# The first pair of heads by unsplit float32 matmuls of 64 rows, and a first value matmul in two pieces

## The chip, the cores and the metric

The kernel runs on 1 core of one Trainium2 chip. The metric is the device time of one execution in microseconds (us), as the median of several runs. Before the change it is 764.4 us, median of 3 runs (762.76 to 766.11).

## What is computed

Attention in which only the keys within `tau` of the row's largest score keep a weight, then a causal convolution of 5 taps that gives a gate, and two 512x512 products. The shapes are 8 batches, 8 heads, 576 positions and 64 numbers per head, all in float32.

```python
scores = scale * np.matmul(q, k.transpose(0, 1, 3, 2))
thresh = np.max(scores, axis=-1, keepdims=True) - tau
scores = np.where(scores >= thresh, scores, -1000000000.0)
attn = softmax(scores)
x = (attn @ v).transpose(0, 2, 1, 3).reshape(B, S, H * D)
gate = sigmoid(causal_conv5(x, conv_w))
out = (gate * (x @ w_val)) @ w_out
```

## The kernel before

The work is cut into 32 jobs, one for each batch and pair of heads (`Job`). A job has nine tiles of scores (`Tile`), each of 128 rows by 576 keys: four query blocks for each of two heads, and one tile, called both, in which the last 64 queries of both heads share the 128 rows. A tile goes through TensorE (scores, `multiply`, L504), VectorE (negative row maximum, L508), ScalarE (exponential L514 and threshold L516) and VectorE again (keep and sum, L530). Two heads of one query block make a `Group`: it is divided by its sum on GpSimd (L560) or ScalarE (L556), turned by TensorE (L610) and copied to SBUF by ScalarE (L621, L626, L632). Five such groups fill two halves of 320 and 256 queries. For each half `Half.attended` (L653) multiplies the turned weights by the values: five key chunks for each of two heads, where head 0 writes partitions 0 to 63 of the result and head 1 partitions 64 to 127. `convolve` and `products` follow (the taps of the first batch on TensorE, L700, the tap of later batches on GpSimd and VectorE, L740 and L747, the two products on TensorE, L794).

A score is not made of one float32 matmul. `prepare` loads q and k of a pair (`q_r`, `k_r`), scales q (L350) and splits both into a high and a low float32r part (L333, L342 on ScalarE, L292 in two pieces each on GpSimd). DMAs then copy the parts within SBUF so that one matmul of 128 rows adds two of the products of parts (`KH`, `KL`, `Q`), and GpSimd places the last 64 queries on a block diagonal (`bd`, L215) for the tile both. Job 0 has a way of its own, `load_at_once`: eight DMAs on two queues bring q and k of both heads twice from HBM, ScalarE makes the high parts (L432, L433) and VectorE the low ones (L438, L440), head by head. `prepare` is called for job 0 as well, for its tile both alone.

The order of the instructions is not that of the text. Every step is an `op` with an engine, a due time, a cost and a list of what it waits for. `carry_out` then plays the engines against each other with those costs and writes the instructions in the order that results. A change to one early step or cost therefore moves instructions all through the program. Buffers are counted rooms (`r_s`: two tiles of scores in PSUM; `r_pre`: two, of which one is lent out at first for the diagonals of the taps).

```python
for c in (NKC, *range(NKC)):
    for h, hs in enumerate(HEADS):
        ...
        nc.tensor.matmul(
            acc[hs, :w], t.v[:, c0 : c0 + D], T[:, chunk, :],
            start=c == NKC, stop=c == NKC - 1, skip_group_check=True,
        )
```

Of the kernel before, what the change touches and what calls it, by code (L numbers as in the profile page):

```python
# [10 lines left out]
F32 = mybir.dt.float32  # L11
# [4 lines left out]
ALU = mybir.AluOpType  # L16
AX = mybir.AxisListType

P = 128
# [3 lines left out]
DUE = (8, 8, 8)  # L23
# [5 lines left out]
def tile_thresholded_attention_gated_mix(  # L29
# [14 lines left out]
    nc = tc.nc  # L44
# [169 lines left out]
    def spread(dst, src):  # L214
        nc.gpsimd.tensor_scalar(dst, src, 1.0, 0.0, op0=ALU.mult, op1=ALU.add)  # L215
# [85 lines left out]
    class Job:  # L301
# [16 lines left out]

        def prepare(self, due):
            b, g = self.b, self.g  # L320
            copy = self.i > 0

            def fetch_k():
                self.k_r = r_kr.take()
                nc.sync.dma_start(self.k_r, kT[b, g])

            def fetch_q():
                self.q_r = r_qr.take()
                nc.sync.dma_start(self.q_r, qT[b, g])

            def high_k():
                self.kh = r_kh.take()
                nc.scalar.copy(self.kh, self.k_r)  # L333

            def low_k():
                if not hasattr(self, "kl"):
                    self.kl = r_kl.take()
                return self.kl, self.k_r, self.kh

            def high_q():  # L340
                self.qh = r_qh.take()
                nc.scalar.copy(self.qh, self.q_r)  # L342

            def low_q():
                if not hasattr(self, "ql"):
                    self.ql = r_ql.take()
                return self.ql, self.q_r, self.qh

            def scale_q():
                nc.gpsimd.tensor_scalar(self.q_r, self.q_r, sc, 0.0, op0=ALU.mult, op1=ALU.add)  # L350

            got_k = op("SP", due - 6, 0.55, 4.0, fetch_k, takes=[r_kr])
            got_q = op("SP", due - 6, 0.55, 4.0, fetch_q, takes=[r_qr])
            self.high_k = op("ACT", due, 0.62, 0.8, high_k, [got_k], [r_kh])
            self.low_k = subtract(due + 1, SK, low_k, [self.high_k], [r_kl], [(r_kr, lambda: self.k_r)])
            scaled = op("POOL", due, 0.75, 0.86, scale_q, [got_q])
            high = op("ACT", due + 1, 0.58, 0.76, high_q, [scaled], [r_qh])
            low = subtract(due + 2, S, low_q, [high], [r_ql], [(r_qr, lambda: self.q_r)])

            def place(which):  # L360
                def run():
                    if which == 0:
                        self.bd = r_bd.take()
                    for hs in HEADS:
                        src = (self.ql if which else self.qh)
                        spread(self.bd[hs, which, hs], src[hs, 0:SL].bitcast(F32))

                return run

            self.blocks = [op("POOL", due + 3, 0.45, 0.6, place(0), [high], [r_bd])]  # L370
            self.blocks.append(op("POOL", due + 3, 0.45, 0.6, place(1), [low, self.blocks[0]]))
            self.give_q = [(r_qh, lambda: self.qh), (r_ql, lambda: self.ql)]
            self.copied = []
            if not copy:
                self.blocks[1].gives = self.give_q
                return

            def copies(name, rooms, src, r):
                def run():
                    if r == 0:  # L380
                        setattr(self, name, rooms.take())
                    dst, x = getattr(self, name), getattr(self, src)
                    for h, hs in enumerate(HEADS):
                        nc.sync.dma_start(
                            dst[HEADS[r], h, :].bitcast(F32), x[hs, self.window(h)].bitcast(F32)
                        )

                return run

            for name, rooms, src, done in (  # L390
                ("KH", r_KH, "kh", self.high_k), ("KL", r_KL, "kl", self.low_k)
            ):
                o = op("SP", due + 1, 1.1, 3.6, copies(name, rooms, src, 0), [done], [rooms])
                o2 = op("SP", due + 1, 1.1, 3.6, copies(name, rooms, src, 1), [done, o])
                self.copied += [o, o2]

            def copies_q(which):
                def run():
                    if which == 0:
                        self.Q = r_Q.take()  # L400
                    x = (self.ql if which else self.qh)
                    for h, hs in enumerate(HEADS):
                        nc.sync.dma_start(
                            self.Q[HEADS[which], h, :].bitcast(F32), x[hs, SL:S].bitcast(F32)
                        )

                return run

            o = op("SP", due + 2, 1.1, 3.6, copies_q(0), [high], [r_Q])
            last = op("SP", due + 2, 1.1, 3.6, copies_q(1), [low, o, *self.blocks],  # L410
                      gives=self.give_q)
            self.copied += [o, last]
# [5 lines left out]
        def load_at_once(self):  # L418

            b, g = self.b, self.g  # L420
            k2, q2 = r_pp.take(), r_pp.take()
            queues = [nc.sync, nc.scalar]
            for h, hs in enumerate(HEADS):
                for r, queue in zip(HEADS, queues):
                    queue.dma_start(k2[r, h * S : (h + 1) * S], kT[b, g, hs, self.window(h)])
                    queue.dma_start(q2[r, h * S : h * S + NKC * P], qT[b, g, hs, SL:S])
            self.Q, self.KH, self.KL = r_Q.take(), r_KH.take(), r_KL.take()
            self.first = []

            def highs(h):  # L430
                k_r, q_r = k2[:, h * S : (h + 1) * S], q2[:, h * S : h * S + NKC * P]
                nc.scalar.copy(self.KH[:, h, :], k_r)  # L432
                nc.scalar.mul(self.Q[:, h, :], q_r, sc)  # L433

            def lows(h):
                k_r, q_r = k2[:, h * S : (h + 1) * S], q2[:, h * S : h * S + NKC * P]
                Q = self.Q[:, h, :]
                nc.vector.tensor_sub(self.KL[:, h, :], k_r, self.KH[:, h, :].bitcast(F32))  # L438
                lo = HEADS[1]
                nc.vector.scalar_tensor_tensor(  # L440
                    Q[lo], q_r[lo], sc[lo], Q[lo].bitcast(F32), op0=ALU.mult, op1=ALU.subtract
                )

            last = []
            for h in range(2):
                last = [op("ACT", -20, 1.3, 1.5, lambda h=h: highs(h), last)]
                low = op("DVEp", -20, 1.5, 1.6, lambda h=h: lows(h), last)
                if h == 1:
                    low.gives = [(r_pp, lambda: k2), (r_pp, lambda: q2)]
                self.first.append(low)  # L450


    class Tile:
        def __init__(self, k, t, h, qc, grp):
# [1 line left out]
            i = h or 0  # L456
            both = h is None
            if both:
                after = [t.high_k, t.low_k, *t.blocks]
            elif t.i == 0:  # L460
                after = [t.first[h]]
            else:
                after = t.copied
            if tiles:
                after = after + [tiles[-1].scores]
            gives = []
            if t.last == (h, qc):
                gives = [(r_Q, lambda: t.Q), (r_KH, lambda: t.KH), (r_KL, lambda: t.KL)]
            if both:
                gives = [(r_kh, lambda: t.kh), (r_kl, lambda: t.kl), (r_bd, lambda: t.bd)]  # L470
            self.scores = op(
                "PE", k - DUE[0], 0.80 if both else 0.54, 1.06 if both else 0.8, self.multiply,
                after, [r_s], gives,
            )
            largest = op("DVE", k - DUE[1], 0.67, 0.84, self.largest, [self.scores], [r_nm])
            if TH == "ACT":
# [14 lines left out]
        def multiply(self):  # L491
            t, h, qc = self.t, self.h, self.qc
            s = self.s = r_s.take()
            for a in range(2):
                hs = slice(a * HS, (a + 1) * HS)
                if h is None:
                    ks = slice(SL + a * HS, SL + (a + 1) * HS)
                    bd = [t.bd[:, i, :] for i in range(2)]
                    terms = [(bd[0], t.kh[:, ks]), (bd[1], t.kh[:, ks]), (bd[0], t.kl[:, ks])]
# [137 lines left out]
    class Half:  # L637
# [4 lines left out]
        def attended(self, k):  # L642
# [3 lines left out]
            def attend():  # L646
                acc = self.acc = r_acc.take()
                T = self.T[:, :, 0:w]
                for c in (NKC, *range(NKC)):
                    for h, hs in enumerate(HEADS):  # L650
                        c0 = (2 * c + h) * D
                        chunk = 2 * NKC if c == NKC else h * NKC + c
                        nc.tensor.matmul(  # L653
                            acc[hs, :w], t.v[:, c0 : c0 + D], T[:, chunk, :],
                            start=c == NKC, stop=c == NKC - 1, skip_group_check=True,
                        )

            def evacuate():
                if j == 0:
# [223 lines left out]
        nc.gpsimd.memset(t.bitcast(F32), 0.0)  # L883
    for _, t in r_xT.free:
        nc.gpsimd.memset(t[:, 0:PAD], 0.0)
    jobs[0].prepare(-6)
    got_cw = op("SP", -20, 0.1, 5.0, lambda: None)
    last, conv_ready = from_f64(
        lambda: cw_raw, lambda: cw_work[0], cw_work[1], cw_work[2], 1, False, [got_cw]
# [80 lines left out]
```

## Time and profile before

| | |
|---|---|
| median of 3 runs | 764.4 us |
| the profiled execution, its own time | 766.08 us |
| its span, first to last instruction | 763.9 us |
| TensorE (PE) busy | 723.8 us, 95% |
| VectorE (DVE), ScalarE (ACT), GpSimd (POOL) busy | 609.8, 637.0, 552.3 us |
| share of PE in the chain that ended last | 72% |
| DMA, mean over the span | 130 GB/s |

Busy is time in which an instruction of the engine was under way. Matmuls overlap, so the pace of TensorE is read from the starts of its instructions, not from their length. In the rows of the trace a bracket tells how long the engine was idle before the instruction and whose work ended that. PEld is the loading of TensorE's weights, SPq and ACTq are instructions that issue DMAs. PEclk is the granted share of TensorE's clock.

### The profile page before, as it was taken

Reading aid. Unit: us, or ns where it says so; the run is one execution under the profiler, and the core shown is the slowest. Engines: PE = TensorE matmul, PEld = TensorE weight load, DVE = VectorE, ACT = ScalarE, POOL = GpSimd, SP = SyncE. Lnnn points to the kernel's source line nnn. Section 1 sums busy time; section 2 is a strip of 40 time slices with the busy share of each in tenths; the row PEclk is TensorE's granted clock in tenths of the full one; section 3 lists DMA queues with packets and bytes.
Section 4 is the critical chain, followed back from the end, with each engine's and each line's share of the span. In section 5 each row is a group of like instructions: output and inputs, shape, how many; then the busy total and the mean of one; then the engine's idle time right before and its main releaser. Section 6 shows DMA issues by size and latency. Waiting matters only on the chain.

```text
span 763.9 us, 16282 instructions
## 1 busy us (share of the span) xinstructions
PE 723.8 (95%) x5424; PEld 617.2 (81%) x5424; DVE 609.8 (80%) x1292; ACT 637.0 (83%) x1466; POOL 552.3 (72%) x908
## 2 busy tenths in 40 slices
PE   3779999999899999999999999999999999999997
PEld 3557678887788888888878888888898888888897
DVE  5796999986788888888788887888888878888730
ACT  5787989988788989888889899888998889988832
POOL 4988778886679867788558976779678777676531
PEclk9999999999899999999999999999999999999999
DMA  6656656446455465654455556545465456550001
GB/s 186 175 144 152 155 133 165 119 116 172 111 142 125 112 165 140 156 127 122 131 131 140 128 143 157 153 104 145 131 161 128 120 141 156 129 125 18 32 33 62
DMA packets 51890, 99.05 MB, mean 130 GB/s; under 512 B 9056, under 2 KB 9056, under 8 KB 51808
## 3 DMA queue, kind: packets, MB, share of 16 engines
q1 hardware_dynamic: 51488, 97.47, 49.8%
q8 instruction: 43, 0.70, 0.4%
q10 hardware_dynamic: 320, 0.56, 0.3%
q14 instruction: 39, 0.32, 0.1%
HBM read 35.74 MB, written 9.44 MB: 59 GB/s over the span
## 4 chain that ended last, share of the span: by engine, by line
PE 72%; DVE 8%; POOL 7%; ACT 6%; issue 3%; DMA 3%; SPq 1%; POOLq 0%; ACTq 0%; DVEq 0%
PE acc L794 20%; PE acc L653 20%; PE s L504 18%; PE tp L610 13%; DVE pp L530 3%; DVE nm L508 2%; ACT e L514 2%; POOL pp L560 2%; ACT T L621 2%; DVE pre L747 1%; DMA q_r<-qT 1%; POOL gl L292 1%; POOL ql L292 1%; PE acc L700 1%; POOL kl L292 1%
## 5 line engine op out<-in xcount | busy, mean ns | idle before, releaser
L508 DVE TENSOR_REDUCE nm<-s 128x1 f32<-128x576 f32 x288 | 216.1, 754 | 61.6 <-PE s L504 56.6
L514 ACT ACTIVATE e<-s,nm 128x576 f32<-128x576 f32 x288 | 215.9, 750 | 33.8 <-DVE nm L508 19.1
L530 DVE SCALAR_TENSOR_TENSOR pp<-s,nm,e 128x576 f32<-128x576 f32 x256 | 207.3, 813 | 36.1 <-ACT nm L516 33.1
L621 ACT COPY T<-tp 128x384 f32<-128x384 f32 x384 | 176.0, 488 | 23.9 <-PE tp L610 22.4
L610 PE MATMUL tp<-ident,pp 128*128 128x128 f32 x1152 | 179.9, 275 | 6.8 <-POOL pp L560 6.4
L504 PE MATMUL s<-KH,Q 128*128 128x288 f32 x512 | 161.0, 330 | 23.1 <-DVE pp L530 13.8
L653 PE MATMUL acc<-T,v 128*64 128x256 f32 (+1 forms) x1280 | 171.0, 414 | 1.5 <-ACT T L621 1.0
L560 POOL TENSOR_SCALAR pp<-pp,sums 128x576 f32<-128x576 f32 x179 | 145.6, 819 | 32.1 <-DVE sums L549 22.3
L610 PEld LDWEIGHTS tp<-ident,pp 128*128 128x128 f32 x1152 | 140.1, 141 | 11.7 <-POOL pp L560 8.2
L504 PE MATMUL s<-KL,Q 128*128 128x288 f32 x512 | 145.0, 298 | 0.0
L653 PEld LDWEIGHTS acc<-T,v 128*64 128x64 f32 x1280 | 86.8, 137 | 63.9 <-issue 7.9
L504 PEld LDWEIGHTS s<-KH,Q 128*128 128x128 f32 x512 | 98.9, 193 | 45.0 <-DVE pp L530 19.4
L747 DVE SCALAR_TENSOR_TENSOR pre<-xT,cw,pre 128x576 f32<-128x576 f32 x112 | 106.2, 948 | 13.2 <-POOL pre L740 12.9
L504 PEld LDWEIGHTS s<-KL,Q 128*128 128x128 f32 x512 | 98.5, 192 | 0.2
L547 POOL TENSOR_SCALAR sums<-sums 128x2 f32<-128x2 f32 (+1 forms) x160 | 48.8, 305 | 57.1 <-DVE pp L530 40.8
L516 ACT ACTIVATE nm<-nm,less 128x1 f32<-128x1 f32 x288 | 85.2, 296 | 0.0
L794 PE MATMUL acc<-gl,woh 128*128 128x320 f32 (+1 forms) x256 | 78.9, 308 | 2.4 <-POOL gl L292 2.4
L794 PE MATMUL acc<-gh,wol 128*128 128x320 f32 (+1 forms) x256 | 79.1, 309 | 0.0
L794 PE MATMUL acc<-gh,woh 128*128 128x320 f32 (+1 forms) x256 | 78.9, 308 | 0.0
L794 PE MATMUL acc<-xh,wvl 128*128 128x320 f32 (+1 forms) x256 | 78.7, 307 | 0.0
L794 PE MATMUL acc<-xl,wvh 128*128 128x320 f32 (+1 forms) x256 | 78.5, 307 | 0.0
L794 PE MATMUL acc<-xh,wvh 128*128 128x320 f32 (+1 forms) x256 | 78.1, 305 | 0.0
(84 smaller groups left out, 1249.0 us busy)
## 6 DMA issues: line engine op xcount, KB each, us to landing
KH<-kh SPq DMA_DIRECT2D x124, 144.0 KB, 2.5
KL<-kl SPq DMA_DIRECT2D x124, 144.0 KB, 3.6
k_r<-kT SPq DMA_DIRECT2D x32, 320.0 KB, 4.0
v<-vs SPq DMA_DIRECT2D x32, 320.0 KB, 3.2
q_r<-qT SPq DMA_DIRECT2D x32, 288.0 KB, 3.4
outT<-o SPq DMA_DIRECT2D x32, 288.0 KB, 2.1
Q<-qh SPq DMA_DIRECT2D x62, 128.0 KB, 2.2
Q<-ql SPq DMA_DIRECT2D x62, 128.0 KB, 2.4
```

What stands on the lines that cost most here:

```text
L504: nc.tensor.matmul(s[:, a, :HS], w, m, start=i == 0, stop=i == len(terms) - 1)
L508: nc.vector.tensor_reduce(self.nm[:, 0:1], self.s[:, :, :HS], axis=AX.XY, op=ALU.max, negate=True)
L514: nc.scalar.activation(self.e, self.s[:, :, :HS], AF.Exp, bias=self.nm[:, 0:1])
L516: nc.scalar.activation(self.nm[:, 1:2], self.nm[:, 0:1], AF.Identity, bias=less, scale=-1.0)
L530: nc.vector.scalar_tensor_tensor(grp.p[:, i * S : (i + 1) * S].rearrange("p (a f) -> p a f", a=2), self.s[:, :, :HS], self.nm[:, 1:2], self.e,
L547: add = op("POOL", k - 4, 0.2, 0.33, lambda: nc.gpsimd.tensor_scalar(sums(), sums(), 1.0, 1e-9, op0=ALU.mult, op1=ALU.add), [self.kept])
L560: nc.gpsimd.tensor_scalar(v, v, ri(i), 0.0, op0=ALU.mult, op1=ALU.add)
L610: nc.tensor.transpose(tp[:, i * P : (i + 1) * P], self.p[:, k0 : k0 + P], ident)
L621: nc.scalar.copy(T[:, c0 : c0 + n, self.off : self.off + P], tp[:, 0 : n * P].rearrange("p (c q) -> p c q", q=P),)
L653: nc.tensor.matmul(acc[hs, :w], t.v[:, c0 : c0 + D], T[:, chunk, :], start=c == NKC, stop=c == NKC - 1, skip_group_check=True,)
L747: nc.vector.scalar_tensor_tensor(cv, t.xT[:, i : i + S], cw[:, g, i : i + 1], cv, op0=ALU.mult, op1=ALU.add)
L794: nc.tensor.matmul(taken[name, e, j][:, :w], wt[:, c, c0 : c0 + P], moving(c, i)[:, hs], start=n == 0, stop=n == NM - 1,)
```

## The change

For job 0 alone, `load_at_once` now makes four DMAs: q and k of head 0 on SP's queue and of head 1 on ACT's, each head in its own 64 partitions of one room of `r_pre`. VectorE scales q (two instructions), GpSimd places the block diagonal, and `multiply` has one float32 matmul for each half of a tile where there were two of float32r (three for the tile both). A matmul of the eight head tiles contracts 64 rows, that of the tile both 128. `prepare` is no longer called for job 0. Its room of `r_pre` is given back after its last tile of scores.

In `attended`, for all 64 halves, the matmul of the first chunk for head 0 is in two pieces: its first 64 queries, then head 1's whole first matmul, then the other queries of head 0.

```diff
             self.blocks.append(op("POOL", due + 3, 0.45, 0.6, place(1), [low, self.blocks[0]]))
             self.give_q = [(r_qh, lambda: self.qh), (r_ql, lambda: self.ql)]
             self.copied = []
-            if not copy:
-                self.blocks[1].gives = self.give_q
-                return
...
         def load_at_once(self):
             b, g = self.b, self.g
-            k2, q2 = r_pp.take(), r_pp.take()
-            queues = [nc.sync, nc.scalar]
-            for h, hs in enumerate(HEADS):
-                for r, queue in zip(HEADS, queues):
-                    queue.dma_start(k2[r, h * S : (h + 1) * S], kT[b, g, hs, self.window(h)])
-                    queue.dma_start(q2[r, h * S : h * S + NKC * P], qT[b, g, hs, SL:S])
...
-            last = []
-            for h in range(2):
-                last = [op("ACT", -20, 1.3, 1.5, lambda h=h: highs(h), last)]
-                low = op("DVEp", -20, 1.5, 1.6, lambda h=h: lows(h), last)
...
+            room = r_pre.take().rearrange("p e s -> p (e s)")
+            self.k, self.q, self.bd = room[:, 0:SK], room[:, SK : SK + S], room[:, SK + S : SK + S + P]
+            for hs, queue in zip(HEADS, (nc.sync, nc.scalar)):
+                queue.dma_start(self.q[hs], qT[b, g, hs])
+                queue.dma_start(self.k[hs], kT[b, g, hs])
+            nc.gpsimd.memset(self.bd, 0.0)
+
+            def scale(hs):
+                nc.vector.tensor_scalar(self.q[hs], self.q[hs], sc[hs], None, op0=ALU.mult)
+
+            def place():
+                for hs in HEADS:
+                    spread(self.bd[hs, hs], self.q[hs, 0:SL])
+
+            self.first = [op("DVEp", -20, 0.36, 0.46, lambda hs=hs: scale(hs)) for hs in HEADS]
+            self.blocks = [op("POOL", -3, 0.45, 0.6, place, self.first)]
+            self.lent = lambda: room.rearrange("p (e s) -> p e s", e=NE)
...
+            cost = 1.0 if t.i == 0 else 0.80 if both else 0.54
             self.scores = op(
-                "PE", k - DUE[0], 0.80 if both else 0.54, 1.06 if both else 0.8, self.multiply,
-                after, [r_s], gives,
+                "PE", k - DUE[0], cost, cost + 0.26, self.multiply, after, [r_s], gives,
             )
...
-                if h is None:
+                if t.i == 0 and h is None:
+                    terms = [(t.bd, t.k[:, SL + a * HS : SL + (a + 1) * HS])]
+                elif t.i == 0:
+                    rows, k0 = HEADS[h], self.t.window(h).start + a * HS
+                    terms = [(t.q[rows, SL + qc * P : SL + (qc + 1) * P], t.k[rows, k0 : k0 + HS])]
+                elif h is None:
...
-                for c in (NKC, *range(NKC)):
-                    for h, hs in enumerate(HEADS):
-                        c0 = (2 * c + h) * D
-                        chunk = 2 * NKC if c == NKC else h * NKC + c
-                        nc.tensor.matmul(
-                            acc[hs, :w], t.v[:, c0 : c0 + D], T[:, chunk, :],
-                            start=c == NKC, stop=c == NKC - 1, skip_group_check=True,
-                        )
+                pieces = [(0, NKC, 0, SL), (1, NKC, 0, w), (0, NKC, SL, w)]
+                pieces += [(h, c, 0, w) for c in range(NKC) for h in range(2)]
+                for n, (h, c, q0, q1) in enumerate(pieces):
+                    c0 = (2 * c + h) * D
+                    chunk = 2 * NKC if c == NKC else h * NKC + c
+                    nc.tensor.matmul(
+                        acc[HEADS[h], q0:q1], t.v[:, c0 : c0 + D], T[:, chunk, q0:q1],
+                        start=n < 2, stop=c == NKC - 1, skip_group_check=True,
+                    )
...
-    jobs[0].prepare(-6)
```

VectorE at the start of the program, before (`KL` and `Q` are the low parts of job 0, `nm` the row maximum of a tile):

```order
L84 TENSOR_SCALAR sc<-tau_sb 128x1
L88 TENSOR_SCALAR less<-tau_sb 128x1
L438 TENSOR_TENSOR KL_119<-pp_129,KH_117 128x576
L440 SCALAR_TENSOR_TENSOR Q_115<-pp_130,sc,Q_115 64x512
L438 TENSOR_TENSOR KL_119<-pp_129,KH_117 128x576
L440 SCALAR_TENSOR_TENSOR Q_115<-pp_130,sc,Q_115 64x512
L508 TENSOR_REDUCE nm_125<-s_101 128x1
L508 TENSOR_REDUCE nm_126<-s_102 128x1
```

and with the change (`pre_154` is the room that holds q and k of job 0):

```order
L84 TENSOR_SCALAR sc<-tau_sb 128x1
L88 TENSOR_SCALAR less<-tau_sb 128x1
L424 TENSOR_SCALAR pre_154<-pre_154,sc 64x576 x2
L497 TENSOR_REDUCE nm_125<-s_101 128x1
L497 TENSOR_REDUCE nm_126<-s_102 128x1
L519 SCALAR_TENSOR_TENSOR pp_129,sums_133<-s_101,nm_125,e_123 128x576
```

Two instructions stand ahead of the first row maximum where there were four.

TensorE at the first half of values in the program (`tp` is a turned block, `acc` the result), before:

```order
L504 MATMUL s_101<-KL_119,Q_115 128x288
L610 MATMUL tp_104<-ident,pl_132 128x128
L653 MATMUL acc_105<-T_138,v_113 64x320 x10
L504 MATMUL s_102<-kh_109,bdq_122 128x288 x2
L504 MATMUL s_102<-kl_110,bdq_122 128x288
```

and with the change:

```order
L599 MATMUL tp_104<-ident,pl_132 128x128
L493 MATMUL s_101<-pre_154 128x288 x2
L643 MATMUL acc_105<-T_138,v_113 64x64
L643 MATMUL acc_105<-T_138,v_113 64x320
L643 MATMUL acc_105<-T_138,v_113 64x256
L643 MATMUL acc_105<-T_138,v_113 64x320 x8
L493 MATMUL s_102<-kh_109,bdq_121 128x288 x2
```

Ten matmuls became eleven, and the tile of scores just ahead has two matmuls where four stood.

SP's queue around the first output of the kernel (`outT`; the `q_r` in this place is that of the tenth job in both programs), before:

```order
L403 DMA Q_116<-ql_112 64x512 x2
L384 DMA KH_117<-kh_109 64x576 x2
L403 DMA Q_115<-qh_111 64x512 x2
L384 DMA KL_119<-kl_110 64x576 x2
L384 DMA KH_117<-kh_109 64x576 x2
L867 DMA outT<-o_166 128x576
L325 DMA k_r_107<-kT 128x640
L329 DMA q_r_108<-qT 128x576
L384 DMA KL_119<-kl_110 64x576 x2
L403 DMA Q_115<-ql_112 64x512 x2
```

and with the change:

```order
L256 DMA o_167<-w_out 128x512
L311 DMA v_114<-vs 128x640
L398 DMA Q_116<-qh_111 64x512 x2
L327 DMA q_r_108<-qT 128x576
L857 DMA outT<-o_166 128x576
L379 DMA KH_118<-kh_109 64x576 x2
L379 DMA KL_120<-kl_110 64x576 x2
L323 DMA k_r_107<-kT 128x640
L379 DMA KH_118<-kh_109 64x576 x2
L379 DMA KL_120<-kl_110 64x576 x2
```

The load of `q_r` moved from behind eight copies, the output and `k_r` to a place ahead of the output and of the copies that follow it.

## Rows read from the trace of the kernel before

**Rows 1.** The page: the chain that ended last, share of the span by engine.

```profile
PE 72%; DVE 8%; POOL 7%; ACT 6%; issue 3%; DMA 3%; SPq 1%; POOLq 0%; ACTq 0%; DVEq 0%
```

**Rows 2.** Stretches: us, busy by engine (instructions), PEclk, DMA share, GB/s.

```profile
7.84:21.50 13.66, 9.53 (x35) 8.12 (x35) 10.16 (x23) 9.32 (x21) 8.69 (x19) 1.00 0.55 174
21.50:55.70 34.20, 25.83 (x175) 20.22 (x177) 30.18 (x70) 27.98 (x68) 29.23 (x52) 1.00 0.68 174
55.70:59.10 3.40, 3.40 (x16) 1.50 (x14) 1.22 (x5) 1.79 (x3) 3.14 (x9) 0.50 0.39 97
192.00:199.00 7.00, 5.83 (x25) 5.79 (x26) 5.15 (x11) 5.18 (x12) 3.84 (x5) 0.51 0.22 45
300.00:400.00 100.00, 98.52 (x763) 84.61 (x762) 83.17 (x171) 85.96 (x200) 72.71 (x116) 1.00 0.51 131
```

**Rows 3.** Timeline of the start, all engines: start us, us, engine, line, operation.

```profile
1.79 0.58 SPq L426 DMA_DIRECT2D pp<-qT  x1
...
6.28 0.72 ACT L433 ACTIVATE Q<-pp,sc 128x512 fp32r<-128x512 f32 x1 [0.29 <-DMA pp<-qT]
...
7.03 0.75 DVE L440 SCALAR_TENSOR_TENSOR Q<-pp,sc,Q 64x512 fp32r<-64x512 f32 x1 [0.25 <-ACT Q L433]
...
7.84 0.61 PE L504 MATMUL s<-KH,Q 128*128 128x288 f32 x1 [7.84 <-DVE Q L440]
...
8.25 0.44 PE L504 MATMUL s<-KL,Q 128*128 128x288 f32 x1
...
8.49 0.44 PE L504 MATMUL s<-KH,Q 128*128 128x288 f32 x1
```

**Rows 4.** Timeline of PE, 22 to 41 us: idle time and its end in brackets.

```profile
23.12 0.55 PE L610 MATMUL tp<-ident,pp 128*128 128x128 f32 x3 [1.85 <-POOL pp L560]
...
27.60 0.29 PE L504 MATMUL s<-KH,Q 128*128 128x288 f32 x1
27.74 0.30 PE L504 MATMUL s<-KL,Q 128*128 128x288 f32 x1
...
28.68 2.91 PE L653 MATMUL acc<-T,v 128*64 128x320 f32 x20 [0.51 <-ACT T L632]
31.52 0.54 PE L504 MATMUL s<-kh,bdq 128*128 128x288 f32 x2
...
33.08 2.32 PE L700 MATMUL acc<-xT,g 128*128 128x320 f32 x8
35.23 0.70 PE L700 MATMUL acc<-xT,pre 128*128 128x320 f32 x2
36.33 0.37 PE L504 MATMUL s<-KH,Q 128*128 128x288 f32 x1 [0.39 <-DMA Q<-ql]
```

**Rows 5.** Timeline at a half of values, 306.8 to 307.1 us, PE and its weight loads.

```profile
306.86 0.20 PEld L653 LDWEIGHTS acc<-T,v 128*64 128x64 f32 x4 [0.16 <-ACT T L621]
306.86 0.49 PE L653 MATMUL acc<-T,v 128*64 128x320 f32 x2
```

**Rows 6.** Timelines of SP, POOL, DVE and PE, 179 to 194 us.

```profile
179.67 0.42 SPq L325 DMA_DIRECT2D k_r<-kT  x1
180.19 0.40 SPq L329 DMA_DIRECT2D q_r<-qT  x1
...
188.14 0.75 POOL L350 TENSOR_SCALAR q_r<-q_r,sc 128x576 f32<-128x576 f32 x1 [4.97 <-DMA q_r<-qT]
...
190.38 1.33 DVE L747 SCALAR_TENSOR_TENSOR pre<-xT,cw,pre 128x576 f32<-128x576 f32 x1 [3.84 <-POOL pre L740]
...
193.17 0.61 PE L504 MATMUL s<-KH,Q 128*128 128x288 f32 x1 [3.88 <-DVE pp L530]
```

**Rows 7.** Timeline of PE, 54 to 60 us.

```profile
54.79 0.55 PE L610 MATMUL tp<-ident,pp 128*128 128x128 f32 x3 [2.81 <-POOL pp L560]
```

**Rows 8.** DMA, 170 to 190 us: KB each, median us to landing.

```profile
Q<-qh SPq DMA_DIRECT2D x2, 128.0 KB, 2.5
...
q_r<-qT SPq DMA_DIRECT2D x1, 288.0 KB, 7.9
```

More of the change, by code (lines that the diff above doesn't have):

```diff
@@ L320, in prepare @@
             b, g = self.b, self.g
-            copy = self.i > 0
             def fetch_k():
@@ L420, in load_at_once @@
             b, g = self.b, self.g
-            k2, q2 = r_pp.take(), r_pp.take()
-            queues = [nc.sync, nc.scalar]
-            for h, hs in enumerate(HEADS):
-                for r, queue in zip(HEADS, queues):
-                    queue.dma_start(k2[r, h * S : (h + 1) * S], kT[b, g, hs, self.window(h)])
-                    queue.dma_start(q2[r, h * S : h * S + NKC * P], qT[b, g, hs, SL:S])
-            self.Q, self.KH, self.KL = r_Q.take(), r_KH.take(), r_KL.take()
-            self.first = []
@@ L430, in highs @@
[L430 to L441, printed above, removed]
-                )
@@ L444, in load_at_once @@
-            last = []
-            for h in range(2):
-                last = [op("ACT", -20, 1.3, 1.5, lambda h=h: highs(h), last)]
-                low = op("DVEp", -20, 1.5, 1.6, lambda h=h: lows(h), last)
-                if h == 1:
-                    low.gives = [(r_pp, lambda: k2), (r_pp, lambda: q2)]
-                self.first.append(low)
+            room = r_pre.take().rearrange("p e s -> p (e s)")
+            self.k, self.q, self.bd = room[:, 0:SK], room[:, SK : SK + S], room[:, SK + S : SK + S + P]
@@ L458, in __init__ @@
             if both:
-                after = [t.high_k, t.low_k, *t.blocks]
+                after = t.blocks if t.i == 0 else [t.high_k, t.low_k, *t.blocks]
             elif t.i == 0:
@@ L466, in __init__ @@
             gives = []
-            if t.last == (h, qc):
+            if t.i == 0:
+                gives = [(r_pre, t.lent)] if t.last == (h, qc) else []
+            elif both:
+                gives = [(r_kh, lambda: t.kh), (r_kl, lambda: t.kl), (r_bd, lambda: t.bd)]
+            elif t.last == (h, qc):
                 gives = [(r_Q, lambda: t.Q), (r_KH, lambda: t.KH), (r_KL, lambda: t.KL)]
-            if both:
-                gives = [(r_kh, lambda: t.kh), (r_kl, lambda: t.kl), (r_bd, lambda: t.bd)]
+            cost = 1.0 if t.i == 0 else 0.80 if both else 0.54
             self.scores = op(
-                "PE", k - DUE[0], 0.80 if both else 0.54, 1.06 if both else 0.8, self.multiply,
-                after, [r_s], gives,
+                "PE", k - DUE[0], cost, cost + 0.26, self.multiply, after, [r_s], gives,
             )
@@ L648, in attend @@
                 T = self.T[:, :, 0:w]
-                for c in (NKC, *range(NKC)):
-                    for h, hs in enumerate(HEADS):
-                        c0 = (2 * c + h) * D
-                        chunk = 2 * NKC if c == NKC else h * NKC + c
-                        nc.tensor.matmul(
-                            acc[hs, :w], t.v[:, c0 : c0 + D], T[:, chunk, :],
-                            start=c == NKC, stop=c == NKC - 1, skip_group_check=True,
-                        )
+                pieces = [(0, NKC, 0, SL), (1, NKC, 0, w), (0, NKC, SL, w)]
[7 more added lines that the diff above has]
+                    )
             def evacuate():
```

## The prediction

> **What bounds the kernel now.** I read the chain that ended last first, then a table of stretches, then the timeline where that table shows TensorE idle. TensorE holds 72% of the chain [rows 1]. From 300 to 400 us it is busy 98.5 of 100 us [rows 2]: there it sets the pace, and a microsecond that its program wins early reaches the end. Early it doesn't set the pace. Its first matmul starts at 7.84 us, released by VectorE's low part of `Q` [rows 3]. From 7.84 to 21.5 us it is busy 9.53 of 13.66 us, from 21.5 to 55.7 us 25.83 of 34.2 [rows 2]. One stall stands apart: at 193.17 us TensorE has been idle for 3.88 us [rows 6], and from 192 to 199 us the clock is granted at 0.51, the lower level (1.2 GHz) [rows 2]. So the change is worth what it does to the first 30 us, to 64 halves of values, and to that stall, since the planner rewrites the order up to there.
>
> **The start.** Eight loads become four; six conversions on ScalarE and four on VectorE become two scalings on VectorE. Today the fourth load of the first wave, issued at 1.79 us on SP, releases ScalarE at 6.28 [rows 3]. In the changed order k of head 0 is the third DMA on SP too, with 160 KB for 128 KB, so I let it land at 6.3 us. The scaling of q is done by then: its q is issued one place earlier, and I bound it between nothing and the 0.75 us of L440, an instruction of the same partitions with one operand more [rows 3]; 0.4 us is nearer to the planner's own cost, and at either end k lands last. TensorE then begins at about 6.4, 1.4 us earlier.
>
> The matmuls are dearer. A float32 matmul is two instructions in the trace (L653 has 20 rows for ten matmuls in the order). Those of L700 with 320 columns start (35.23 - 33.08) / 8 = 0.269 us apart [rows 4], so with 288 columns 0.24 us, or 0.48 at the lower clock. A head tile takes four of them: 0.97 us, or 1.9. Today it takes four float32r instructions of 0.14 us at full clock (27.60 to 27.74) [rows 4] and of 0.24 at 8.25 us [rows 3], where half as fast means the lower level although the clock's row reads 1.00. So nine tiles cost 9 x 0.97 = 8.7 us at full clock, and 17.3 at the lower one, against 8 x 0.55 + 0.8 = 5.2 and 10.4 today (0.8 is six float32r instructions).
>
> Most of this isn't on the path. With two rooms of scores the third tile waits for VectorE to keep the first, and the tile's VectorE work, about 1.6 us, is longer than 0.97. Gone at the same time are job 0's two pieces each of `kl` and `ql`, its scaling and its block diagonals on GpSimd, besides the ten conversions; GpSimd does job 1's in that place, so job 1 is ready earlier. Two things pay: TensorE waits 1.85 us for a division on GpSimd at 23.12 us, behind such work, and in the new order the divisions of the second group stand ahead of the diagonals of the taps; and the wait of 0.39 us for a copy of job 1's `Q` at 36.33 [rows 4] has its cover back. I take the first half of values (28.68 us today [rows 4]) 2.1 us earlier: 1.4 of the start and 0.7 of these waits, nearest to the row of the start, and 0.4 for `Q`. Bounds: at the lower clock throughout, the nine tiles end at 6.4 + 17.3 = 23.7 us, which leaves 5.0 us until 28.68 for turning the groups, so the lead is nothing; if both kinds of waits vanish, 1.4 + 1.85 + 0.39 = 3.6 us. Between 64-row and full matmuls the array may also pause, which I price from the halves of values below at under 0.2 us each, inside these bounds. The Trainium skill, page TensorEngine Tiling (Array Packing), section Key Properties, says that changing the tiling mode drains the engine; by that, eight such changes would cost an estimated 1.4 us.
>
> **The two pieces.** A half of 320 queries takes 31.52 - 28.68 = 2.84 us for 20 instructions [rows 4], 0.142 each, where an instruction with as many columns alone takes 0.269. So two run side by side, and two start within 0.01 us at 306.86 [rows 5]: head 0 and head 1, in different halves of the array's columns. Four weight loads are under way in the first 0.2 us there, so a load is ready before the matmul that needs it. The change adds two instructions to head 0's row of ten and no columns. If each head's row runs on by itself, the cost is an instruction's overhead twice. I estimate it from 0.269 us less the 0.267 that 320 columns, streamed twice at 2.4 GHz, would take: 2 x 0.002, in 64 halves 0.3 us. Bounds: nothing, and 8.5 us (below).
>
> **The stall at 193 us.** SP issues `q_r` at 180.19 us behind eight copies, an output and `k_r`; it takes 7.9 us to land where a `Q` copy a little earlier took 2.5 [rows 6, 8]. GpSimd waits 4.97 us for it with a division and a tap queued behind, VectorE 3.84 us for the tap, TensorE 3.88 us for VectorE [rows 6]. The clock then costs half of about 6.9 us, 3.4 more [rows 2]: 7.3 us together. In the new order this load stands ahead of the output and of the copies of the next job, so this jam should go: -7.3. But new orders make new meetings. The next stall of the sort is the 2.81 us at 54.79 [rows 7] with 3.4 us at clock 0.50 behind it [rows 2], half of that lost: 4.5 us. I book one such stall as added somewhere, between nothing and a full 7.3 us.
>
> **Sum:** -2.1 - 0.4 + 0.3 - 7.3 + 4.5 = -5.0 us. The profiled execution took 766.08 us, 1.7 above the median of the three runs, and the steps hold for either: 761.1 against its own time, **759.4 us** against the median. Below 0.5% (3.8 us) a measurement of this kernel can't tell a difference from none.
>
> **Rivals.**
> - *The jam only moves.* The start wins its 2.1 + 0.4 us, but the planner doesn't know how long transfers queue, and the same number of bytes passes; a jam as dear comes elsewhere in the first 200 us. 764.4 - 2.2 = 762.2, no change to speak of. For it: seven DMAs still follow the output closely in the new order. Chance 0.25.
> - *The pieces lock.* If the matmuls of the two heads must start in the program's order, head 0's second piece can't start before head 1's second pass. Head 0's two short passes end after 2 x 0.054 us (0.269 x 64 / 320), head 1's first after 0.269, so head 0 idles 0.16 us in a half of 320 queries and 0.215 - 0.108 = 0.107 in one of 256: 32 x 0.267 = 8.5 us, all where TensorE sets the pace. With the jam staying, 762.2 - 0.3 + 8.5 = 770.4, slower; with it gone 767.6. It decides from about 0.08 us a half on, where it eats the 5 us of the sum. Against it: side by side today, head 1's first pass starts with head 0's first although head 0's second stands between them in the program. For it: the rows don't say which head an instruction belongs to. Chance 0.13. The Trainium skill's page TensorE: Matmul & The Clock Gate, Part 3, section "What overlaps and what doesn't", says that matmuls start and end strictly in program order; by that, this rival holds, and the pairs of rows 5 speak against it only if they are the two heads.
> - *Slow tiles eat the lead.* The clock stays at the lower level to 21.5 us as today, and 1.9 us a tile becomes the pace of job 0. Lead nothing, the rest as in the sum: 759.4 + 2.5 = 761.9; with the jam moved, 764.7. For it: today's clock rises only after 21 us. Against it: TensorE is less often idle. Chance 0.10.
> - *Worse meetings.* Two jams of the size at 193 us replace one: 762.2 + 7.3 = 769.5. Chance 0.10.
>
> **How the numbers follow.** The forecast, jam gone with at most one smaller stall (754.9 to 759.4), has 0.42. Faster by over 0.5% (under 760.6) are the forecast and 0.05 of the rivals in which a lead of 3.6 us meets a cheap jam: 0.47. Slower (over 768.2) are the worse meetings, the pieces lock with the jam staying (0.06) and 0.02 of tails: 0.18. The rest, 0.35, is no change. The range takes in the sum without a new stall, 754.9, with 1.1 more of lead, and on the other side 770.4: 753 to 770. The likeliest case has 753 to 761 for itself.
>
> **What would show it.** The first matmul starts at about 6.4 us and the first half of values near 26.6. A half of 320 queries still takes 2.84 us and one of 256 is as much unchanged; 3.0 us shows the pieces locking. No wait of GpSimd for `q_r` of 5 us near 180 us, no low clock there. The prediction is wrong if TensorE's idle time from 60 to 200 us is as large as today while the start moved as said, or if a half's length changed by over 0.05 us.

## The result and the profile after

The changed kernel takes **755.4 us** (median of 6 runs, 753.16 to 757.69), the kernel before beside it 764.65 (6 runs, 762.76 to 766.11): a ratio of 0.987, 95% interval [0.986, 0.989], 9.3 us faster. The forecast was 759.4 us in a range of 753 to 770, and faster by over 0.5% was its likeliest case, so it was right by its numbers. By its reasons it was right on the first matmul, the pieces and the stall at 193 us, wrong on the lead at the first half of values and on the stall that it booked as added. It also missed what the experiments below show: that the work of the change is not what wins the 9 us. Four other orders of the old work win 5 to 13 us without it.

The page after: busy time by engine, and the chain that ended last.

```profile
PE 728.2 (96%) x5550; PEld 624.9 (83%) x5550; DVE 601.5 (80%) x1290; ACT 639.4 (85%) x1470; POOL 539.7 (71%) x892
...
PE 84%; DVE 5%; ACT 4%; POOL 3%; DMA 1%; issue 1%; SPq 0%; POOLq 0%; ACTq 0%
```

The profiled execution took 756.97 us with a span of 755.2. TensorE holds 84% of the chain where it held 72% [rows 1]. Its busy time rose by 4.4 us, and the span is still 8.7 us shorter: TensorE does more and waits less.

Stretches after, in the columns of rows 2. The second and third are the places of the two stalls of before.

```profile
6.21:30.40 24.19, 18.13 (x59) 11.61 (x59) 13.03 (x32) 14.03 (x32) 13.68 (x35) 0.95 0.56 159
...
55.70:59.10 3.40, 3.40 (x26) 2.30 (x28) 2.38 (x7) 2.88 (x8) 2.94 (x6) 1.00 0.22 72
192.00:199.00 7.00, 7.00 (x56) 5.47 (x55) 5.83 (x14) 6.89 (x15) 5.81 (x11) 1.00 0.58 163
300.00:400.00 100.00, 99.91 (x794) 87.49 (x794) 83.28 (x175) 90.89 (x209) 76.94 (x127) 1.00 0.56 141
```

The stall at 193 us is gone, and of the one at 54.79 us a wait of 1.12 us is left (at 55.70). The low clock behind both is gone: 0.50 and 0.51 before [rows 2], 1.00 now. From 300 to 400 us TensorE is busy 99.9 us for 98.5. The first line runs from the first matmul to the first half of values. The same stretch before:

```profile
7.84:28.68 20.84, 13.11 (x62) 11.24 (x62) 17.31 (x40) 15.56 (x36) 14.78 (x30) 1.00 0.57 160
```

TensorE was busy 13.11 of 20.84 us there and is busy 18.13 of 24.19 now. So it waits 1.7 us less (6.06 for 7.73) and works 5.0 us more, and although it begins 1.63 us earlier it reaches the first half of values 1.72 us later, at 30.40 us for 28.68.

PE's timeline after, 6 to 36 us.

```profile
6.21 2.39 PE L493 MATMUL s<-pre 64*128 64x288 f32 x8 [6.21 <-DMA pre<-kT]
11.13 3.10 PE L493 MATMUL s<-pre 64*128 64x288 f32 x8 [2.53 <-DVE pp L519]
16.04 0.87 PE L599 MATMUL tp<-ident,pp 128*128 128x128 f32 x3 [1.81 <-POOL kl L292]
16.71 2.13 PE L493 MATMUL s<-pre 128*128 128x288 f32 x4
18.63 1.49 PE L599 MATMUL tp<-ident,pp 128*128 128x128 f32 x6
20.05 1.70 PE L493 MATMUL s<-pre 64*128 64x288 f32 x4
21.68 0.94 PE L599 MATMUL tp<-ident,pp 128*128 128x128 f32 x6
23.33 1.23 PE L493 MATMUL s<-pre 64*128 64x288 f32 x4 [0.72 <-DVE pl L519]
24.49 0.55 PE L599 MATMUL tp<-ident,pp 128*128 128x128 f32 x3
24.97 1.24 PE L493 MATMUL s<-pre 64*128 64x288 f32 x4
26.14 0.66 PE L599 MATMUL tp<-ident,pl 128*128 128x128 f32 x4
27.80 0.47 PE L599 MATMUL tp<-ident,pl 128*128 128x128 f32 x1 [1.00 <-POOL pl L215]
28.19 2.28 PE L493 MATMUL s<-pre 64*128 64x288 f32 x4
30.40 5.00 PE L643 MATMUL acc<-T,v 128*64 128x64 f32 x22
35.34 0.53 PE L493 MATMUL s<-kh,bdq 128*128 128x288 f32 x2
```

The first line is as forecast: k of head 0 releases TensorE at 6.21 us. Then the dear tiles follow, 14.1 us by the seven groups of `s<-pre`, where the nine tiles of before had 10.4, by the same reckoning from first start to last end; so the tiles are 3.7 of the 5.0 us. The half at 30.40 takes 4.94 us to the next matmul, not 2.84: the clock was granted at its lower level (1.2 GHz) from about 28 to 35 us.

How far ahead the changed kernel is can be read at the start of a half of values in both traces (before, and after minus before):

| half | before, us | difference, us |
|---|---|---|
| 1st | 28.68 | +1.7 |
| 5th | 81.08 | -2.1 |
| 14th | 182.58 | -2.4 |
| 17th | 221.43 | -10.0 |
| 64th | 728.70 | -8.7 |

So 3.9 us come between the first and the fifth half (TensorE waits 3.3 us there for 6.9, and both traces have a spell of the lower clock there), 7.6 us between the 14th and the 17th, where before had its stall at 193 us, and 1.3 us are lost again later.

SP's queue after, where `q_r` of the tenth job is issued.

```profile
164.46 2.06 SPq L398 DMA_DIRECT2D Q<-qh  x2
166.66 0.49 SPq L327 DMA_DIRECT2D q_r<-qT  x1
168.50 0.35 SPq L857 DMA_DIRECT2D outT<-o  x1
172.12 1.11 SPq L379 DMA_DIRECT2D KH<-kh  x2
```

The DMAs after, 160 to 190 us: KB each, median us to landing.

```profile
q_r<-qT SPq DMA_DIRECT2D x1, 288.0 KB, 2.9
```

`q_r` now goes out at 166.66 us, ahead of the output and the copies, and lands in 2.9 us for 7.9 [rows 8].

### The profile page after: what moved, and what is told of

Its sections match the earlier page's. It is cut to its first block, busy times and chain, and to the rows that moved or that the text cites. A ratio compares the mean times of both kernels' runs of the same rounds, so it can differ in the third digit from the quotient of the medians.

```text
span 755.2 us, 16467 instructions
## 1 busy us (share of the span) xinstructions
PE 728.2 (96%) x5550; PEld 624.9 (83%) x5550; DVE 601.5 (80%) x1290; ACT 639.4 (85%) x1470; POOL 539.7 (71%) x892
## 4 chain that ended last, share of the span: by engine, by line
PE 84%; DVE 5%; ACT 4%; POOL 3%; DMA 1%; issue 1%; SPq 0%; POOLq 0%; ACTq 0%
PE acc L784 24%; PE acc L643 21%; PE s L493 21%; PE tp L599 17%; DVE nm L497 2%; PE acc L690 2%; DVE pp L519 2%; ACT e L503 1%; ACT T L610 1%; DMA q_r<-qT 1%; POOL gl L292 1%; DMA pre<-kT 1%; POOL pp L549 1%; DVE pre L737 0%; ACT xh L720 0%
## 5 line engine op out<-in xcount | busy, mean ns | idle before, releaser
L643 PE MATMUL acc<-T,v 128*64 128x256 f32 (+3 forms) x1408 | 172.4, 393 | 0.3 <-ACT T L610 0.2
L549 POOL TENSOR_SCALAR pp<-pp,sums 128x576 f32<-128x576 f32 x172 | 142.6, 834 | 40.4 <-DVE sums L538 30.2
L493 PE MATMUL s<-KH,Q 128*128 128x288 f32 x496 | 154.1, 326 | 4.2 <-DVE pp L519 3.8
L643 PEld LDWEIGHTS acc<-T,v 128*64 128x64 f32 x1408 | 97.1, 138 | 54.4 <-issue 10.7
L493 PE MATMUL s<-KL,Q 128*128 128x288 f32 x496 | 138.7, 295 | 0.0
L493 PEld LDWEIGHTS s<-KH,Q 128*128 128x128 f32 x496 | 94.4, 190 | 25.9 <-DVE pp L519 9.0
L493 PEld LDWEIGHTS s<-KL,Q 128*128 128x128 f32 x496 | 93.9, 189 | 0.2
L536 POOL TENSOR_SCALAR sums<-sums 128x2 f32<-128x2 f32 (+1 forms) x160 | 45.6, 285 | 58.2 <-DVE pp L519 36.4
```

The source lines that it names most:

```text
L493: nc.tensor.matmul(s[:, a, :HS], w, m, start=i == 0, stop=i == len(terms) - 1)
L536: add = op("POOL", k - 4, 0.2, 0.33, lambda: nc.gpsimd.tensor_scalar(sums(), sums(), 1.0, 1e-9, op0=ALU.mult, op1=ALU.add), [self.kept])
L549: nc.gpsimd.tensor_scalar(v, v, ri(i), 0.0, op0=ALU.mult, op1=ALU.add)
L643: nc.tensor.matmul(acc[HEADS[h], q0:q1], t.v[:, c0 : c0 + D], T[:, chunk, q0:q1], start=n < 2, stop=c == NKC - 1, skip_group_check=True,)
```

## The experiments

Each was timed in three rounds beside the kernel before. In these rounds the kernel before took 765.4 to 765.7 us.

**The pieces, each way.** In `whole_first` the changed kernel has its first value matmul whole again, in `pieces_alone` the kernel before has only the pieces. Neither moves an instruction otherwise.

```diff
-    pieces = [(0, NKC, 0, SL), (1, NKC, 0, w), (0, NKC, SL, w)]
-    pieces += [(h, c, 0, w) for c in range(NKC) for h in range(2)]
+    for c in (NKC, *range(NKC)):
+        for h, hs in enumerate(HEADS):
...
```

> The changed kernel, but with the first value matmul of head 0 whole again, so that 64 x 2 instructions fewer run and the planner's order is the same. If the pieces cost an instruction's overhead alone: 0.3 us less than the changed kernel, 755.1 us, and 2.842 us for a half of 320 queries. If the pieces are what made the change faster: 2 us or more slower, 757.5 us or above.

> The kernel before with the first value matmul of head 0 in two pieces and nothing else; the order is that of before. If the pieces are neutral: 764.9 us, 2.846 us a half of 320 queries. If they bring the gain: 757 us or less.

`whole_first` took 756.2 us, 0.988 [0.985, 0.991] of before, as the changed kernel; `pieces_alone` 766.6, 1.0007 [0.9996, 1.0018] of before. The pieces cost nothing that can be measured, and they win nothing. In the traces a half of 320 queries from 200 us on takes 2.846 us with the pieces and 2.843 without (medians of 24 or 25 halves whose next matmul follows without a wait), one of 256 2.313 and 2.310. One half of 320 queries in PE's timeline after:

```profile
317.38 2.92 PE L643 MATMUL acc<-T,v 128*64 128x64 f32 x22
320.23 0.39 PE L784 MATMUL acc<-xl,wvh 128*128 128x256 f32 x1
```

The matmuls of `acc` in that half that begin from 317.3 to 317.7 us: count, shortest/median/longest ns, first and last start, shapes.

```profile
L643 PE MATMUL acc<-T,v x4: 222/326/484, 317.4 to 317.5; 128*64 128x64 f32 x2, 128*64 128x320 f32 x1, 128*64 128x256 f32 x1
```

From 317.38 to 320.23 it takes 2.85 us. Four instructions have begun by 317.55: both passes of head 0's first piece (64), one pass of head 1 (320), and one of head 0's second piece (256). The second pass of head 1, which stands between the last two in the program, begins later, 0.33 us into the half. So each head's row runs on by itself, and the rival of the locked pieces falls.

`whole_first` has the order of the changed kernel, and in its profiled execution the clock, once risen, kept its upper level up to the first half of values:

```profile
6.12:28.42 22.30, 16.38 (x59) 10.60 (x59) 13.02 (x32) 13.88 (x32) 12.58 (x32) 1.00 0.65 173
```

The same instructions keep TensorE busy for 16.38 us here and for 18.13 in the changed kernel, and the first half begins at 28.42 us.

**The stall at 193 us alone.** The kernel before with the copies of one job's parts cut to 8 columns each, so that the queue ahead of `q_r` is short. The scores of the ninth job are then made from old data; the rest is computed as before.

```diff
+    m = 8 if self.i == 8 else S
...
-    dst[HEADS[r], h, :].bitcast(F32), x[hs, self.window(h)].bitcast(F32)
+    dst[HEADS[r], h, 0:m].bitcast(F32), x[hs, self.window(h)][:, 0:m].bitcast(F32)
```

> The kernel before, with the twelve copies within SBUF of the ninth job cut to 8 columns each (its scores are then taken from old data), the order unchanged: the load of q of the tenth job no longer stands behind 1.1 MB. If that queue makes the stall at 193 us: q lands in about 3 us, no idle time of 3.9 us and no lower clock at 192 to 199 us, 7.3 us less, 757.4 us. If the stall has another cause or the time is lost elsewhere anyway: 763 us or more.

It took 760.6 us, 0.994 [0.992, 0.996], 4.9 us less than before. `q_r` lands in 4.6 us for 7.9 [rows 8] (about 3 was expected), and GpSimd waits 1.38 us for it, where it waited 4.97 [rows 6]:

```profile
183.97 0.75 POOL L350 TENSOR_SCALAR q_r<-q_r,sc 128x576 f32<-128x576 f32 x1 [1.38 <-DMA q_r<-qT]
```

Its stretches at the old stall and at a spell of low clock:

```profile
192.00:199.00 7.00, 7.00 (x54) 5.37 (x53) 5.27 (x12) 6.33 (x14) 6.39 (x12) 1.00 0.46 115
104.00:108.40 4.40, 4.40 (x22) 2.04 (x20) 3.25 (x10) 2.52 (x5) 4.13 (x8) 0.61 0.59 136
```

The copies around `q_r` on the queue were the cause of the stall: with them short, TensorE is busy 7.00 of 7.00 us at the full clock. Eight of the twelve stand ahead of `q_r` and four behind it; this run doesn't part the two. From the 14th to the 17th half the trace takes 33.0 us (181.98 to 215.01) for 38.9 before, so the stall was worth 5.8 us and not the 7.3 that I had summed. A part of that sum was counted twice: the low clock begins at 192.2 us, while TensorE still waits until 193.17, and from 192 to 199 us it was busy 5.83 of 7 us [rows 2]; half of that is 2.9, and 3.88 + 2.9 = 6.8. The low clock at 104 us is no effect of the edit, since the first short copy goes out at 172.96 us.

**The same work in another order.** If the stall went only because the order is another one, then any new order might do it. So one cost in the planner was moved by 0.01 (two in order_4), in the kernel before and in the changed one. No instruction is added or taken away, but the planner also chooses the engine of a division: of 288, GpSimd has 209 in the kernel before, 194, 195, 193 and 205 in its orders 1 to 4, 199 in the changed kernel and 194 to 201 in its new orders. An order means this whole plan here. With only four divisions moved, order_4 wins as much as order_2 does with 14, so that share alone isn't what decides.

In order_1:

```diff
-            largest = op("DVE", k - DUE[1], 0.67, 0.84, self.largest, [self.scores], [r_nm])
+            largest = op("DVE", k - DUE[1], 0.68, 0.85, self.largest, [self.scores], [r_nm])
```

In order_2, and in order_4:

```diff
-                "DVE", k - DUE[2], 0.74, 0.96, self.keep, after, room + ([] if i else [r_sums]),
+                "DVE", k - DUE[2], 0.75, 0.97, self.keep, after, room + ([] if i else [r_sums]),
```

In order_3, and in order_4:

```diff
-                after = [op("ACT", k - DUE[1], 0.83, 1.0, self.weigh, [largest], [r_e])]
+                after = [op("ACT", k - DUE[1], 0.82, 0.99, self.weigh, [largest], [r_e])]
```

> The kernel before with one cost of the planner changed by 0.01 us (the row maximum, 0.67 to 0.68), so the same work in another order. If the order alone decides whether such stalls occur: any time from 755 to 770 us, unlike 764.7 by more than 2 us in at least one of three such kernels. If the changed kernel won by its lighter start: within 1.5 us of 764.7.

> As before_order_1 with another cost (the keeping of a tile on VectorE, 0.74 to 0.75). Order theory: unlike 764.7 us by over 2 us in at least one of the three. Start theory: within 1.5 us of it.

> As before_order_1 with another cost (the exponential on ScalarE, 0.83 to 0.82). Order theory: unlike 764.7 us by over 2 us in at least one of the three. Start theory: within 1.5 us of it.

> The changed kernel with the planner's cost of the row maximum at 0.68 for 0.67: the same work as the changed kernel in another order. Order theory: scattered by several us around a mean that differs little from the mean of the three re-ordered kernels of before. Start theory: within 1.5 us of 755.4, so 9 us under its twin.

> As after_order_1 with the keeping of a tile at 0.75 for 0.74. Order theory: scattered, the mean near that of the re-ordered kernels of before. Start theory: within 1.5 us of 755.4.

> The kernel before with two of the planner's costs moved by 0.01 (exponential 0.82, keep and sum 0.75): the same work, a fourth new order. Theory that the gain is luck of the order: 752 to 762 us, as the three others (760.1, 754.3, 752.8), and again below the kernel before. Rival, that the order of before is ordinary and the three others were lucky: 763 us or more.

> The changed kernel with the planner's cost of the exponential lowered from 0.83 to 0.82 (1.0 to 0.99): the same work in another order; the same edit took the kernel before to 752.8 us. Theory that the gain is luck of the order: the time lies anywhere among those of the re-ordered kernels, 752 to 763 us, and not near 755.4 by right. Rival, that the change saves work at the start: about 2 to 9 us below the kernel before in the same edit, 744 to 751 us.

> The changed kernel with the same two costs moved. Theory of the order: 752 to 763 us, with no fixed lead on the kernel before in the same edit. Rival, that the change saves work: 2 to 9 us below that kernel.

Medians in us, with the ratio to the kernel before and its interval:

| planner's costs | work of before | work of the change | change minus before |
|---|---|---|---|
| as they were | 764.65 | 755.4, 0.987 [0.986, 0.989] | -9.3 |
| order_1 | 760.1, 0.992 [0.989, 0.995] | 761.8, 0.995 [0.993, 0.997] | +1.7 |
| order_2 | 754.3, 0.985 [0.983, 0.986] | 762.4, 0.997 [0.995, 0.998] | +8.1 |
| order_3 | 752.8, 0.983 [0.981, 0.984] | 757.4, 0.989 [0.988, 0.991] | +4.6 |
| order_4 | 754.1, 0.986 [0.983, 0.988] | 758.6, 0.991 [0.989, 0.994] | +4.4 |

The work of before is faster in each of four new orders, by 5.3 to 13.0 us against the kernel before in the same rounds, with nothing of the change in it. The work of the change has a higher median in each of four new orders, and with equal costs it is slower than the work of before by 1.7 to 8.1 us, 4.7 in the mean; in order_1 the intervals overlap. Equal costs don't give both kernels the same order, so each line compares two draws, and with the first line counted the mean is 1.9. The expectation that the two means would lie close together was not met. The order that the kernel before happened to have is the slowest of its five; the one that the change happened to get is the fastest of its five. `before_order_3` is the fastest kernel here, 13.0 us under the kernel before of its rounds and 2.6 under the changed one, and the intervals of the two ratios don't overlap.

Its stretches, from the first matmul to the first half of values and at the two places of the stalls:

```profile
8.18:29.54 21.36, 14.66 (x62) 12.34 (x62) 17.81 (x42) 16.48 (x38) 15.03 (x30) 0.92 0.57 167
55.70:59.10 3.40, 2.95 (x22) 1.91 (x23) 2.86 (x9) 3.40 (x8) 3.23 (x9) 1.00 0.02 5
192.00:199.00 7.00, 7.00 (x57) 7.00 (x56) 5.13 (x11) 6.47 (x16) 5.46 (x8) 1.00 0.54 141
```

It reaches the first half later than before (29.54 us), so nothing is won at the start, and the stall at 193 us is gone as in the changed kernel. All four new orders of the work of before have TensorE busy 7.00 of 7.00 us there, at clock 1.00.

The pages of the profiled executions tell what an order brings and what the work costs (idle is the span less TensorE's busy time):

| us | span | TensorE busy | TensorE idle |
|---|---|---|---|
| the kernel before | 763.9 | 723.8 | 40.1 |
| its four new orders | 750.9 to 754.5 | 720.2 to 723.3 | 30.3 to 32.4 |
| the changed kernel | 755.2 | 728.2 | 27.0 |
| its four new orders | 756.0 to 763.7 | 726.7 to 733.7 | 29.3 to 31.5 |

The four new orders take 8 to 10 us of waiting away without the change. In the means of the four, the work of the change saves 1.3 us of waiting and adds 7.5 us of busy time. Part of the 7.5 can be the clock, since the same work is busy for longer at the lower level: `whole_first`, without such a spell after its start, has 723.5.

`after_order_1` shows what an order can bring back. Its PE timeline:

```profile
150.07 0.31 PE L784 MATMUL acc<-xh,wvl 128*128 128x320 f32 x1
154.04 0.45 PE L493 MATMUL s<-KH,Q 128*128 128x288 f32 x1 [3.66 <-DVE pp L519]
```

The stretch behind it:

```profile
154.00:157.40 3.40, 3.36 (x16) 2.19 (x18) 3.21 (x9) 2.99 (x7) 1.52 (x2) 0.54 0.58 154
```

That is a stall of the same size in another place: 3.66 us of waiting, then the lower clock. Its cause is another one. VectorE, for which TensorE waits, is never idle from 147.4 to 154 us; taps and conversions of weights stand in its queue ahead of the keeping of the tile (the last line) that frees TensorE's room, and it waits for no load:

```profile
150.71 1.00 DVE L234 SCALAR_TENSOR_TENSOR spare<-woh,spare 128x256 f32<-128x256 f32 x1
151.64 1.41 DVE L737 SCALAR_TENSOR_TENSOR pre<-xT,cw,pre 128x576 f32<-128x576 f32 x1
152.97 0.28 DVE L236 TENSOR_SCALAR spare_m<-spare 128x256 int32<-128x256 int32 x1
153.17 0.81 DVE L519 SCALAR_TENSOR_TENSOR pp<-s,nm,e 128x576 f32<-128x576 f32 x1
```

It is a "new meeting" such as the prediction booked, and it costs 3.66 + 1.7 (half of 3.4) = 5.4 us; this kernel is 6.4 us slower than the changed one.

**The dear tiles alone.** The changed kernel in its own order, with each float32 matmul of job 0's scores issued twice; the second overwrites the first with the same numbers.

```diff
+    for _ in range(2 if t.i == 0 else 1):
         for i, (w, m) in enumerate(terms):
             nc.tensor.matmul(s[:, a, :HS], w, m, start=i == 0, stop=i == len(terms) - 1)
```

> The changed kernel in its own order, but every float32 matmul of scores of job 0 is issued twice (the second overwrites the first with the same numbers, so the output is the same). That adds some 9 tiles of 1 us to TensorE, more at the lower clock. Theory that VectorE sets the pace in job 0 and covers the dearer matmuls: at most 2 us more than the changed kernel, 755 to 758 us. Rival, that TensorE's work there is on the path: 4 to 10 us more, 760 to 766 us.

It took 762.1 us, 0.996 [0.994, 0.997] of before and 6.7 us more than the changed kernel by the medians (5.8, if each is taken against the kernel before of its rounds). The theory that VectorE covers these matmuls falls. Its PE timeline at the start:

```profile
6.12 6.26 PE L494 MATMUL s<-pre 64*128 64x288 f32 x16 [6.12 <-DMA pre<-kT]
14.10 5.58 PE L494 MATMUL s<-pre 64*128 64x288 f32 x16 [1.71 <-DVE pp L520]
...
24.11 2.20 PE L494 MATMUL s<-pre 64*128 64x288 f32 x8
```

The stretch from its first matmul to its first half of values:

```profile
6.12:36.44 30.32, 25.69 (x96) 17.92 (x96) 13.30 (x33) 14.08 (x33) 15.01 (x39) 1.00 0.46 128
```

TensorE is busy 7.6 us longer ahead of the first half (25.69 for 18.13) and reaches it 6.0 us later (36.44 for 30.40). Four fifths of what is added to TensorE there comes through. Against `whole_first`, which has no spell of the lower clock there either, it is 9.3 us of busy time and 8.0 us of delay. At the end 6 to 7 us are still there.

## Why the prediction was right, and where it was not

- **The first matmul at 6.4 us:** right, 6.21, released by k of head 0 as said.
- **The lead of 2.1 us at the first half of values:** wrong, and this is the step that failed. It came 1.7 us later in the profiled execution and 0.3 earlier in that of `whole_first`, whose clock, once risen, kept its upper level; so about 2 us of the miss are the clock in one execution, and 1.8 are there without it. The size of the added work was about right: 3.5 to 6.9 us more by the clock was the estimate for the tiles, and the rows have 3.7 more (2.2 in `whole_first`). What failed is the sentence "most of this isn't on the path". It took the tile's VectorE work as the pace. But TensorE was busy 13.11 of 20.84 us, and the rest is a handful of single waits, as the one of 1.85 us in rows 4; work added between two waits pushes all that follows, and `double_scores` measures it. The rival "slow tiles eat the lead" described this step better and had 0.10. One part I had not foreseen at all softened it: at 6.21 us two tiles take 2.39 us together, not 2 x 1.9 (last section).
- **The waits, 0.7 and 0.4 us:** right in direction, too small, and partly wrong in place. TensorE waits 1.7 us less ahead of the first half. The wait for the second group's division is gone (its turning begins at 21.68 without a wait) and so is the one for `Q`, but before the first group's turning there is a longer one (1.81 us at 16.04 for 0.88 us at 16.69 before; put down to `kl`, with ScalarE's division ending at 15.90), and a new one of 1.00 us at 27.80 stands behind the diagonals of the taps on GpSimd.
- **The pieces, 0.3 us:** right. 64 x 0.003 us is 0.2. The page TensorE: Matmul & The Clock Gate of the Trainium skill (Part 3, "What overlaps and what doesn't") has matmuls start strictly in program order. By that rule, if the two passes of each matmul count as two in the program, a half would have grown by 0.11 to 0.16 us, and it grew by 0.003: here the measurement decides against the rule so read, for matmuls that go to different halves of the array's columns.
- **The stall at 193 us, -7.3:** right in mechanism; in this order 7.6 us come between the 14th and the 17th half. Taken away by itself it gave 5.8 us there and 4.9 by the medians; the 7.3 counted about a microsecond of waiting at the low clock twice.
- **The new stall, +4.5:** wrong for this order. Not one stall of that size was added, and the one at 54.79 went too for the most part (1.12 us of waiting at 55.70 for 2.81, full clock behind it). The step drew one sample of what a new order brings and charged it; `after_order_1` is a kernel in which the charge fell due.
- **The sum:** -5.0 was forecast and -9.3 came. The difference is the start (+1.7 for -2.5) against the two stalls (7.6 + 3.9 for 7.3 - 4.5). That these misses have opposite signs is luck: the first alone would have made it -0.8, the second alone -13.4, below the range.

What the prediction didn't say, and should have: it ascribed the gain of 7.3 us to the change, when each of the four new orders of the unchanged work takes the stall away too. Over the four new orders the work of the change itself comes out at +4.7 us in the mean, and the pages show it as TensorE's busy time. The starts of the halves don't show it: at the first half three of the pairs are 3 to 6 us apart (35.50 for 29.36, 32.91 for 29.54, 32.91 for 29.84 us, with 69 instructions ahead of it for 61 or 62), but not at the fifth (79.24 for 80.84, 79.44 for 80.81, 78.78 for 78.37), since a new order also moves work from one side of a half to the other. Whether 4.7 us is the price in general stays open: four orders spread over 1.7 to 8.1, and the one pair of the original costs has -9.3.

## What to carry to other kernels

Where a planner sets the order, a change of any early step draws a new order, and the spread among orders of the same work (12 us here) can be larger than what the step is worth: before crediting a change, shift a planner's cost by 0.01 in both kernels and time them in several such pairs, since one pair is one draw. And judge added work at the start by whether TensorE has room between its waits there, not by which engine has the longest work per tile: 7.6 us added to TensorE came through as 6.0.

## What the runs showed of the hardware

- **Two float32 tiles of 64 rows run side by side.** Head 0's q and k are on partitions 0 to 63, head 1's on 64 to 127. In the trace after, the eight matmul instructions of the two tiles at 6.21 us begin in pairs 0.14 us apart, and from the second pair on 0.48 us after the last; the group takes 2.39 us, when one such tile alone takes 2.28 us at 28.19, at the same lower clock. The Trainium skill's page TensorE: Matmul & The Clock Gate, Part 3, says that small matmuls in different row tiles of the array run at the same time; the trace agrees, and the working of the prediction had left it out.
- **The lower clock comes and goes between executions of like kernels.** From 28 to 35 us it was there in the changed kernel, and not in `whole_first`, which has the same order; a half of values took 4.94 us under it for 2.84.
- **A switch between 64-row tiles and whole ones costs 0.2 us or less.** One such tile between transposes takes 1.17 us (24.97 to 26.14 us) where its four matmul instructions, 0.24 us apart, make 0.97. The step from the last transpose to the tile is longer too (0.20 us for 0.11 between two transposes), and so is the first step behind it (0.17 for 0.11), so the two switches cost 0.35 us at most, 0.2 of them within the tile. The Trainium skill, TensorEngine Tiling (Array Packing), Key Properties, says that a change of mode drains the engine; the prediction's estimate of 1.4 us for eight changes would be 0.35 for two, at this bound, but no run here measures the drain by itself.
